# Pooling maxima through DRAM instead of a diagonal and a product with ones, and a new list of pieces

## The chip, the cores and the metric

One core of a Trainium2 chip runs the whole program. The metric is device time in microseconds of one execution; a kernel is told by the median of its runs. Engines: TensorE (PE, its weight loads PEld), VectorE (DVE), ScalarE (ACT), GpSimd (POOL) and SyncE (SP), which issues nearly all DMA transfers.

## The reference

Attention with pooled keys and values for 8 batches of 8 heads, then a two-layer network on the 4608 rows of its result:

```python
a = softmax(phi, axis=2)                    # phi: 8 x 8 x 576 x 32
k_m = einsum('bhsm,bhsd->bhmd', a, k)       # 32 pooled keys a head
v_m = einsum('bhsm,bhsd->bhmd', a, v)
attn = softmax(q @ k_m.T / sqrt(64)) @ v_m  # over the 32
x = attn as 4608 x 512
h = x @ w_in                                # 512 x 2048
out = (h - tanh(h)) @ w_out                 # 2048 x 512
```

The program's softmax of phi first needs, for each of the 256 columns (8 heads of 32) of a batch, the maximum over the 576 positions: it is subtracted from phi ahead of the exponential.

## The kernel before, in words

The work is cut into pieces, and a string, ORDER, lists every piece by hand or by a planner as a word; a loop runs through it, and each engine gets its instructions in just that order. A word is a letter for the step, then its indices; a step of several parts (Python `yield`) is named once for each part. "i0:gg", "o3:gg", "k1:q" are loads of blocks of w_in, w_out, or of a block to be checked, into a buffer whose name stands behind the colon. A trailing x takes the other PSUM buffer. SP's transfers too are issued in the list's order: an issue waits until the buffer is free and until the data are there, and what stands behind it on SP waits with it.

The words that matter here, with b a batch, t a half of its positions, u a unit of 256 rows, f a fourth of the 2048 columns:

- FX b, FQ b load phi with columns on partitions (`pt`), FA b loads it with positions on partitions (`e`); KA, KB, KR load keys and values, Q, QT load queries.
- X b: VectorE takes the maxima `mx` (128 partitions x 2) of `pt`. For batches 0 and 1 another way is used, which the change leaves alone. For batches 2 to 7 it also makes `dg`, the identity times the maxima (L193).
- XP b: TensorE multiplies ones by `dg` (L202), which puts the 256 maxima into every partition of a PSUM tile, `pmx`.
- Y b (batches 2, 3) subtracts `pmx` from `e` on VectorE (L210, L213); YM b (batches 4 to 7) copies it to SBUF as `ms` on ScalarE (L221) and subtracts on GpSimd. YE b is the exponential on ScalarE (L226).
- V b pools keys and values with `e` (L271, L279), N b divides, U b and UV b turn the result; S b.t are the scores, AM, AE, AD, AT, AS the second softmax and its split into a high and a low f16 half (L351 to L564); a "v" behind AM, AD, AS, c, s, L, SS or CW (and Ev) moves a step from GpSimd or ScalarE to VectorE.
- P b.f folds the pooled values into w_in (L573); H u.f is the first layer's product (L622); a or ap, g, c, f, s turn it into f16 parts of h - tanh(h) (L629 to L693); M u.f is the second layer's product (L750 for the first units, L769 for the rest), E or Ev adds up and stores.
- T p turns blocks of float64 weights, read as integers, into f32 and f16 on VectorE (L447, L450, L453) and ScalarE (L464); L, Lv, Lp make the low half. Z are products that only keep TensorE busy.

Of the kernel before, what the change touches and what calls it, by code (L numbers as in the profile page):

```python
# [83 lines left out]
AMv2.0 PL1.3 M0.2 L14 c1.3 c0.3 H2.2 H2.2 AMv2.0 AM2.1 AM2.1 a2.2 AE2.0 ADv2.0 P2.0 a2.2 H2.3 H2.3 a2.3 M1.2 M1.2 PL2.0 a2.2 BF0 g2.2 cv2.2 H3.2 L15
P2.1 H3.2 L14 M1.3 a2.3 a2.3 BH0 BL0 M1.3 ADv2.0 W2 AT2.0 ap3.2 P2.1 R1 O1 O1 AE2.1 ap3.2 ap3.2 PL2.1 BS1 BF1 AS2.0 AS2.0 M0.3 M0.3 H4.0 H4.0 ap4.0 R0
P2.2 H3.3 g2.3 c2.3 O0 O0 BH1 BL1 AD2.1 AD2.1 ap4.0 ap4.0 M2.2 R2 X3 g3.2 c3.2 P2.2 PL2.2 H3.3 H4.1 H4.1 ap3.3 ap3.3 g4.0 ap4.1 ap4.1 KR3.0 XP3 Y3
f4.0 s4.0 M2.2 QT3.0 ap3.3 g3.3 s4.0 YE3 cv4.0 M2.3 M2.3 H4.2 O2 O2 c3.3 ap4.1 AT2.1 R3 H4.2 BS2 P2.3 AS2.1 P2.3 g4.1 AS2.1 V3.0x PL2.3 ap4.2 ap4.2
BF2 BH2 M3.2 f4.1 ap4.2 f4.2 M3.2 H4.3x s4.1 KR3.1 s4.1 BL2 V3.1 N3 k4:q XX M3.3 M3.3 H4.3 ap4.3 ap4.3 g4.2 U3x U3 UV3 M4.0 M4.0 cv4.1 UV3 S3.0x ap4.3
O3 O3 P3.0 M4.0 M4.0 S3.0 AMv3.0 P3.0 M4.1 H5.0 BS3 AMv3.0 AE3.0 f4.3 k0:e g4.3 cv4.3 M4.1 M4.1 M4.1 PL3.0 c4.2 s4.2 s4.2 P3.1 H5.0 a5.0 a5.0 M4.2
sv4.3 H5.1 CW4 BF3 a5.0 BH3 BL3 H5.1 g5.0 k2:q c5.0 M4.2 M4.2 f5.0 QT3.1 M4.2 H5.2 s5.0 sv4.3 M4.3 P3.1 a5.1 ADv3.0 a5.1 M4.3 M4.3 PL3.1 S3.1 ADv3.0  # L90
s5.0 a5.1 AT3.0 M4.3 H5.2 S3.1 E4 g5.1 a5.2 a5.2 E4 CW2 f5.1 E4 E4 sv5.1 P3.2 M4.3 H5.3 H5.3 FQ4 M5.0 FA4 M5.0 a5.2 cv5.1 E4 E4 AS3.0 a5.3 sv5.1 M5.0
M5.0 CW0 AS3.0 H6.0 M5.1 M5.1 M5.1 M5.1 f5.2 a5.3 g5.2 KR4.0 cv5.2 s5.2 s5.2 a5.3 H6.0 a6.0 f5.3 a6.0 a6.0 P3.2 H6.1 s5.3 H6.1 f6.0 M5.2 M5.2 M5.2
M5.2 P3.3 g5.3 c5.3 s5.3 M5.3 ap6.1 ap6.1 PL3.2 H6.2 ap6.1 g6.1 P3.3 AM3.1 AM3.1 c6.1 AE3.1 X4 XP4 g6.0 M5.3 c6.0 s6.0 PL3.3 f6.1 H6.2 a6.2 KR4.1 M5.3
Ev5 Ev5 M5.3 s6.0 Ev5 Ev5 Ev5 a6.2 ADv3.1 ADv3.1 YM4 M5.3 s6.1 Ev5 a6.2 YM4 YE4 H6.3 H6.3 s6.1 QT4.0 AT3.1 ap6.3 ap6.3 M6.0 M6.0 AS3.1 AS3.1 g6.2 k3:e
f6.2 M6.0 sv6.2 V4.0 M6.1 M6.1 ap6.3 g6.3 f6.3 M6.0 M6.1 M6.1 sv6.3 sv6.2 H7.0 H7.0 a7.0 c6.2 V4.1 N4 W3 a7.0 sv6.3 M6.2 SI0 H7.1 a7.0 f7.0 H7.1 a7.1
U4 UV4 FQ5 UV4 M6.2 QT4.1 M6.2 a7.1 M6.2 U4 H7.2 H7.2 SSv0 NI0 a7.1 f7.1 a7.2 c6.3 M6.3 NI0 g7.0 a7.2 a7.2 s7.0 S4.0 c7.0 S4.0 AMv4.0 M6.3 M6.3 E6
s7.0 g7.2 c7.2 H7.3 H7.3 E6 a7.3 M6.3 E6 s7.1 E6 E6 W4 g7.1 M6.3 E6 s7.1 P4.0 P4.0 S4.1x S4.1 AMv4.1 a7.3 X5 CW3 AMv4.0 AE4.0 a7.3 g7.3 M7.0 M7.0 M7.0
M7.0 H8.0 H8.0 f7.2 c7.1 M7.1 M7.1 M7.1 M7.1 s7.2 f7.3 PL4.0 ap8.0 ap8.0 AMv4.1 AD4.0 ap8.0 XP5 s7.2 k5:e sv7.3 CW5 cv7.3 M7.2 KR5.0 AD4.0 f8.0 g8.0
M7.2 M7.2 M7.2 sv7.3 AE4.1 ADv4.1 s8.0 s8.0 c8.0 AT4.0 H8.1 YM5 ADv4.1 H8.1 P4.1 P4.1 M7.3 M7.3 a8.1 a8.1 a8.1 H8.2 AS4.0 PL4.1 M7.3 Ev7 H8.2 a8.2 FA5
QT5.0 YM5 a8.2 YE5 f8.1 M7.3 Ev7 P4.2 P4.2 g8.1 M7.3 AS4.0 c8.1 s8.1 s8.1 Ev7 Ev7 a8.2 g8.2 Ev7 H8.3 M8.0 Ev7 M8.0 c8.2 M8.0 V5.0 M8.1 AT4.1 AS4.1  # L100
KR5.1 PL4.2 H9.0 H8.3 a8.3 a8.3 a8.3 H9.0 f8.2 a9.0 a9.0 s8.2 s8.2 M8.1 M8.1 V5.1 f8.3 P4.3x P4.3 N5 s8.3 k6:e M8.0 M8.1 g8.3 H9.1x H9.1 a9.0 PL4.3
U5x s8.3 UV5 ap9.1 f9.0 M8.2 M8.2 UV5 ap9.1 ap9.1 c8.3 f9.1 M8.2 M8.2 M8.3 g9.0 c9.0 M8.3 SI1 k7:q SS1 U5 S5.0 g9.1 M8.3 sv9.0 k8:e E8 E8 H9.2 E8 E8
S5.0 M8.3 M8.3 AS4.1 H9.2 H9.3x sv9.0 CW6 ap9.2 ap9.2 ap9.2 QT5.1 c9.1 M9.0 M9.0 M9.0 E8 E8 s9.1 s9.1 AM5.0 H9.3 a9.3 AM5.0 f9.2 a9.3 FQ6 a9.3 NI1x
NI1 AE5.0 AD5.0 AD5.0 H10.0x H10.0 M9.1 M9.1 a10.0 s9.2 P5.0 f9.3 S5.1x a10.0 g9.2 P5.0 c9.2 a10.0 M9.0 M9.1 H10.1 s9.2 CW8 M9.1 M9.2 g9.3 c9.3 S5.1
AMv5.1 AMv5.1 AE5.1 M9.2 M9.2 M9.2 AT5.0 AS5.0 X6 XP6 s9.3 H10.1 s9.3 M9.3 PL5.0 ap10.1 H10.2 AS5.0 ADv5.1 ap10.1 ap10.1 g10.1 f10.1 g10.0 YM6 f10.0
H10.2 a10.2 FA6 P5.1 P5.1 c10.0 CW7 YM6 PL5.1 M9.3 a10.2 a10.2 QT6.0 M9.3 M9.3 M9.3 s10.0 E9 E9 s10.1 H10.3x KR6.0 H10.3 H11.0 cv10.1 a10.3 E9 E9 E9
E9 a10.3 a10.3 YE6 P5.2 P5.2 s10.0 M10.0 M10.0 M10.0 KR6.1 V6.0 H11.0 PL5.2 a11.0 H11.1 k10:q a11.0 s10.1 f10.2 s10.2 M10.0 M10.1 g10.2 a11.0 H11.1
# [1033 lines left out]
```

## Time and profile before

| | |
|---|---|
| median of 3 runs | 635.8 us (635.18 to 636.08) |
| the profiled execution | 636.29 us, span 634.2 us |
| busy, share of the span | PE 98%, DVE 90%, ACT 68%, POOL 55% |
| mean granted TensorE clock | 0.996 |

A row tells a line of the kernel, the engine, the operation, tiles written <- tiles read, and shape. Busy times of matmuls overlap their neighbours, so a product's place in TensorE's queue is read from the start of the next one.

### The profile page before, as it was taken

To read this page: it belongs to the slowest core of one execution; us is meant where nothing else is said; L and a number is where in the kernel's file an instruction comes from. 1 tells how busy PE (TensorE), PEld (TensorE's weight loads), DVE (VectorE), ACT (ScalarE), POOL (GpSimd) and SP (SyncE) were. 2 spreads that over 40 slices of the span, in tenths; PEclk is the share of its full clock that TensorE was granted. 3 is DMA by queue.
4 is the path that set the end of the run, shared out by engine and by line. 5 is a ranking of instruction groups with operands and counts; after the bars stand their busy time and mean duration, and the time that the engine had idled before them with its cause. 6 is when DMAs were issued, how large, how long until landed. Compare 5 with 4: busy or idle time off the path is not lost.

```text
span 634.2 us, 16291 instructions
## 1 busy us (share of the span) xinstructions
PE 619.4 (98%) x6908; PEld 485.5 (77%) x6908; DVE 570.9 (90%) x763; ACT 428.7 (68%) x601; POOL 350.5 (55%) x314
## 2 busy tenths in 40 slices
...
GB/s 342 416 269 274 252 264 158 118 73 68 184 138 145 65 56 72 73 167 112 116 85 122 113 67 149 109 88 173 38 41 163 118 103 89 49 153 35 166 100 39
DMA packets 25872, 85.03 MB, mean 134 GB/s; under 512 B 2752, under 2 KB 2752, under 8 KB 25024
## 3 DMA queue, kind: packets, MB, share of 16 engines
...
HBM read 72.37 MB, written 11.53 MB: 132 GB/s over the span
## 4 chain that ended last, share of the span: by engine, by line
PE 86%; DVE 7%; DMA 4%; ACT 1%; issue 1%; SPq 0%; DVEq 0%; ACTq 0%
PE h L622 27%; PE x L769 22%; PE o L769 16%; PE o L750 10%; PE pp L573 3%; PE o1h L750 3%; DMA raw<-in_w_out_dram 3%; PE pkv L271 2%; DMA pt<-in_phx_dram 1%; PE psc L323 1%; DVE h L642 1%; DVE wt L450 1%; DVE wt L453 1%; DVE h L646 1%; DVE bw L709 0%
## 5 line engine op out<-in xcount | busy, mean ns | idle before, releaser
L622 PE MATMUL h<-ah,ph 128*128 128x256 f16 (+3 forms) x1536 | 201.0, 246 | 0.7 <-DVE h L642 0.7
L622 PEld LDWEIGHTS <-ph 128*128 128x128 f16 x2304 | 178.2, 98 | 20.7 <-issue 3.7
L672 POOL TENSOR_TENSOR g<-h,g 128x512 f16<-128x512 f32 x114 | 128.3, 1147 | 100.4 <-ACT g L666 94.2
L622 PE MATMUL h<-al,ph 128*128 128x256 f16 (+3 forms) x768 | 170.0, 246 | 1.1 <-POOL al L564 1.1
L693 POOL TENSOR_TENSOR f<-s,f 128x512 f16<-128x512 f32 x86 | 107.3, 1269 | 86.1 <-ACT f L689 81.1
L769 PEld LDWEIGHTS <-f 128*128 128x128 f16 x1344 | 129.1, 98 | 20.8 <-issue 5.2
L769 PE MATMUL x<-bt,f 128*128 128x256 f16 x1008 | 128.3, 273 | 0.0
L644 ACT ACTIVATE u<-u,beta 128x1024 f32<-128x1024 f32 x72 | 82.5, 1146 | 46.8 <-DVE h L642 46.5
L769 PEld LDWEIGHTS <-g 128*128 128x128 f16 x1008 | 97.9, 98 | 14.7 <-issue 3.5
L629 ACT ACTIVATE u<-h 128x1024 f32<-128x1024 f32 x72 | 73.3, 1018 | 47.6 <-PE h L622 31.4
L642 DVE SCALAR_TENSOR_TENSOR h<-h,u 128x1024 f32<-128x1024 f32 x72 | 87.9, 1221 | 19.2 <-ACT u L629 17.6
L646 DVE SCALAR_TENSOR_TENSOR h<-u,h 128x1024 f32<-128x1024 f32 x72 | 92.7, 1289 | 11.7 <-ACT u L644 11.4
L666 ACT ACTIVATE g<-h 128x512 f16<-128x512 f32 (+2 forms) x128 | 68.2, 579 | 19.9 <-DVE h L646 13.4
L750 PEld LDWEIGHTS <-g 128*128 128x128 f16 x384 | 36.7, 98 | 45.2 <-issue 3.0
L689 ACT ACTIVATE f<-s 128x1024 f16<-128x1024 f32 x56 | 58.6, 1048 | 11.1 <-DVE s L682 7.0
L750 PE MATMUL o<-wout_hi,g 128*128 128x512 f16 x192 | 59.0, 379 | 0.0
L680 DVE TENSOR_TENSOR s<-h 128x512 f32<-128x512 f32 x56 | 45.3, 808 | 2.0 <-DVE h L646 0.5
L769 PE MATMUL o<-wout_hi,f 128*128 128x256 f16 x224 | 45.9, 273 | 0.0
L769 PE MATMUL o<-wout_hi,g 128*128 128x256 f16 x224 | 45.8, 273 | 0.0
L769 PE MATMUL x<-wout_hi,g 128*128 128x256 f16 x224 | 45.8, 273 | 0.0
L769 PE MATMUL o<-bt,g 128*128 128x256 f16 x336 | 45.3, 273 | 0.0
L586 ACT ACTIVATE ph<-pp 128x1024 f16<-128x1024 f32 x32 | 32.4, 1014 | 18.4 <-PE pp L573 17.6
...
## 6 DMA issues: line engine op xcount, KB each, us to landing
...
chk<-in_w_in_dram SPq DMA_DIRECT2D x16, 512.0 KB, 4.1
chk<-in_w_out_dram SPq DMA_DIRECT2D x16, 512.0 KB, 3.8
...
kv<-in_kva_dram SPq DMA_DIRECT2D x6, 1032.0 KB, 9.7
...
raw<-in_w_out_dram SPq DMA_DIRECT2D x12, 512.0 KB, 8.6
```

The lines of the kernel that those rows point to most:

```text
L622: nc.tensor.matmul(hp[:, k, tu : tu + w], px[:, g, cs], d[ax][:, g, ta : ta + w], start=(n == 0), stop=(n == 5),)
L629: nc.scalar.activation(uu, hp, AF.Square, scale=1.0 / (S_A * S_P))
L642: nc.vector.scalar_tensor_tensor(t, hp, C2 * S_G / (S_A * S_P), uu, op0=ALU.mult, op1=ALU.mult)
L644: nc.scalar.activation(uu, uu, AF.Square, bias=c["beta"])
L646: nc.vector.scalar_tensor_tensor(h3, uu, CC, t, op0=ALU.add, op1=ALU.mult)
L666: nc.scalar.activation(hi, x, AF.Copy)
L672: eng.tensor_tensor(lo[:, ks], x[:, ks], hi[:, ks], op=ALU.subtract)
L680: nc.vector.tensor_tensor(s[:, 0:2], pair, a_block(h3, 0, 0).unsqueeze(1).to_broadcast((P, 2, 2, P)), op=ALU.add)
L689: nc.scalar.activation(f[:, 0], s, AF.Copy)
L693: eng.tensor_tensor(f[:, 1, ks], s[:, ks], f[:, 0, ks], op=ALU.subtract)
L750: nc.tensor.matmul(o, gx[:, k, P * tt : P * tt + P], wx[:, 4 * fb + k, :], start=(first and k == 0 and wx is wout_hi and gx is gh), stop=( ...
L769: nc.tensor.matmul(dst, a(na, kk), b(nb, kk), start=(new and kk == 0 and na == 0 and nb == 0), stop=(end and kk == 1 and na == 1))
```

## The change

The maxima of batches 2 to 7 go to a DRAM tile of 2 x 128, and from there to all partitions of an SBUF tile `ms` of their own; the diagonal, the product with ones, its PSUM tile and ScalarE's copy go. Y and YM both subtract `ms`. Both transfers are issued by SP, at X and at XP.

```diff
-        dg = big.tile([P, 2, P], F32, tag="qt", name=f"dg{b}", bufs=1)
-        nc.vector.tensor_tensor(
-            dg, self.c["ident"].unsqueeze(1).to_broadcast((P, 2, P)),
-            mx.unsqueeze(2).to_broadcast((P, 2, P)), op=ALU.mult,
-        )
-        d["dg"] = dg
-
-    def top_all(self, b, d, early=False):
-        nc, dg = self.tc.nc, d["dg"]
-        pa = self.psum(f"pmx{b}", early)
-        nc.tensor.matmul(pa[:, 0, 0:256], self.c["ones"], dg.rearrange("p a b -> p (a b)"), start=True, stop=True)
-        d["px"] = pa
+        d["md"] = self.dram.tile([2, P], F32, tag=f"md{b}", name=f"md{b}")
+        nc.sync.dma_start(d["md"].rearrange("r p -> p r"), mx)
+
+    def top_all(self, b, d):
+        d["ms"] = m = self.big.tile([P, 256], F32, tag="ms", name=f"ms{b}", bufs=1)
+        row = d["md"].rearrange("r p -> (r p)").unsqueeze(0).to_broadcast((P, 256))
+        self.tc.nc.sync.dma_start(m, row)
...
-    def expo(self, b, d):
-        self.less_top(self.tc.nc.vector, d["e"], d["px"][:, 0, 0:256])
-
-    def expo_pool(self, b, d):
-
-        m = self.big.tile([P, 256], F32, tag="qt", name=f"ms{b}", bufs=1)
-        self.tc.nc.scalar.activation(m, d["px"][:, 0, 0:256], AF.Copy)
-        yield
-        self.less_top(self.tc.nc.gpsimd, d["e"], m)
+    def expo(self, b, d, eng=None):
+        self.less_top(eng or self.tc.nc.vector, d["e"], d["ms"])
```

The list is replaced as a whole (1710 words before, 1707 after). The same pieces are in it; many stand elsewhere, and some have moved between engines. To VectorE: AS 0.0, 1.0, 2.0, 2.1, 3.1, 6.1, 7.1; AM 1.1, 3.1, 6.0, 6.1; AD 1.1, 5.0, 6.1; L2, SS1; c 2.0, 7.2, 8.1, 10.2, 11.3, 12.0, 12.1 and eight s. Away from it: AS 7.0; AM 2.0, 4.0; AD 2.0, 3.1; L4, L7; c 0.1, 4.0, 4.1, 5.1, 7.3, 10.1, 12.3, 14.3, 16.0 and seven s; E5, E7, E11 for E4 and E15. From the start of the second batch's softmax, and around batch 2's maxima, it reads:

```diff
-H0.0x ASv0.1 T10 ASv0.1 H1.0 Lp9 T10 T10 L10 o6:gg o7:gg H1.1 H0.0
+ASv0.0 ASv0.0 o6:gg H0.0x AT0.1 Lp9 T10 ASv0.1 ASv0.1 H1.0 H1.1 Z0.0 Z0.0 H0.0 KA1 o7:gg T10 T10 T11 T11 FX1 X1
...
-AT1.1 T5 OP1 OP1 FA2 T5 T4 L5 L5 Q2.0 H2.0x H2.0 cv0.1 M0.1 AS1.1 T4 KB2 M0.1 T4 T4 PL1.1 H2.1 FX2 a2.0 a2.0 X2 XP2 o8:gg AS1.1 H3.0 OP0 OP0 H2.1 a2.0
-g2.0 M2.0 i12:kv2 T12 T12 T12 Y2 a2.1 CW1 H3.0 c2.0 T12 a2.1 Lv4 o11:gg T13 T13 P0.2 P0.2 M2.0 a2.1 H3.1 i14:kv3 g2.1 KA2 c2.1 ap3.0 FA3 PL0.2 YE2
-Lv12 ap3.0 ap3.0 V2.0 V2.1
+OP1 OP1 T5 T5 T4 L5 PL1.0 L5 ASv1.0 H2.0 H2.0 T4 T4 OP0 FA2 M0.1 FX2 X2 PL1.1 H2.1x ap2.0 o10:pp5 XP2 Q2.1 T4 ap2.0 L4 o11:gg H2.1 AS1.1 H3.0 OP0 L4
+P0.2 T12 T12 T12 ap2.0 g2.0 M2.0 H3.1 a2.1 Y2 a2.1 a2.1 cv2.0 H3.0 g2.1 KA2 a3.0 P0.2 PL0.2 T13 YE2 V2.0 V2.1
```

## Rows read from the trace of the kernel before

**Rows 1.** The page of the profile: span and instructions; busy time, share of the span and instructions of each engine; and the chain that ended last, its shares by engine.

```profile
span 634.2 us, 16291 instructions
...
PE 619.4 (98%) x6908; PEld 485.5 (77%) x6908; DVE 570.9 (90%) x763; ACT 428.7 (68%) x601; POOL 350.5 (55%) x314
...
PE 86%; DVE 7%; DMA 4%; ACT 1%; issue 1%; SPq 0%; DVEq 0%; ACTq 0%
```

**Rows 2.** Busy time of each engine (with the number of instructions) in four stretches of the span; after them the granted TensorE clock, the DMA engines' mean busy share and GB/s.

```profile
0.00:60.00 60.00, 51.31 (x522) 28.70 (x522) 49.46 (x80) 38.55 (x51) 17.76 (x28) 0.97 0.83 326
60.00:200.00 140.00, 140.00 (x1457) 86.42 (x1456) 136.70 (x162) 91.80 (x112) 73.73 (x55) 1.00 0.44 154
200.00:560.00 360.00, 358.73 (x4309) 308.51 (x4294) 327.58 (x439) 252.53 (x371) 223.15 (x199) 1.00 0.31 104
560.00:634.20 74.20, 69.31 (x639) 61.89 (x637) 57.16 (x85) 45.79 (x69) 35.87 (x34) 0.99 0.25 87
```

**Rows 3.** The timeline of TensorE's matmuls around three of the XP products (start, us; us until the end of the last one merged; line, operation, tiles, shape, count).

```profile
83.17 0.62 PE L202 MATMUL pmx<-dg,ones 128*128 128x256 f32 x2
83.63 0.27 PE L622 MATMUL h<-ah,ph 128*128 128x256 f16 x1
83.74 0.27 PE L622 MATMUL h<-al,ph 128*128 128x256 f16 x1
...
169.52 0.65 PE L202 MATMUL pmx<-dg,ones 128*128 128x256 f32 x2
170.00 0.38 PE L750 MATMUL o<-wout_hi,g 128*128 128x512 f16 x1
...
448.78 0.60 PE L202 MATMUL pmx<-dg,ones 128*128 128x256 f32 x2
449.21 0.38 PE L769 MATMUL x<-bt,f 128*128 128x256 f16 x2
```

**Rows 4.** The chain that ended last in the first 80 us, its two long loads (start, us); and the timeline from 22 to 40 us (an idle time before an instruction and what ended it in brackets).

```profile
10.43 14.39 DMA raw<-in_w_out_dram
...
40.51 5.65 DMA raw<-in_w_out_dram
...
22.83 0.16 DVE L284 TENSOR_SCALAR kr<-pkv 128x2 f32<-128x2 f32 x1 [2.07 <-PE pkv L279]
...
36.07 1.39 POOL L564 TENSOR_TENSOR al<-af,ah 128x576 f16<-128x576 f32 x1 [0.36 <-ACT ah L562]
...
37.51 0.27 PE L622 MATMUL h<-al,ph 128*128 128x256 f16 x1 [1.11 <-POOL al L564]
...
34.97 1.36 DVE L447 TENSOR_SCALAR wt<-raw 128x512 uint32<-128x512 uint32 x2
36.24 0.77 DVE L373 STREAM_TRANSPOSE af<-sc 128x576 f32<-128x576 f32 x1
36.94 1.67 DVE L450 SCALAR_TENSOR_TENSOR wt<-raw,wt 128x512 uint32<-128x512 uint32 x2
38.53 0.75 DVE L564 TENSOR_TENSOR al<-af,ah 128x576 f16<-128x576 f32 x1
```

**Rows 5.** Groups of TensorE's matmuls, shapes apart: count, busy us, mean ns of one, idle time before.

```profile
L858 PE MATMUL warm<-nid 128*128 128x512 f16 x52 | 13.7, 411 | 1.9 <-DVE nid L1086 1.9
```

**Rows 6.** Instructions by tile: the diagonal dg, the exponential on e and the copy ms (duration in ns min/median/max, first and last start).

```profile
L193 DVE TENSOR_TENSOR dg<-ident,mx x6: 424/444/1099, 80.5 to 440.0; 128x256 f32<-128x256 f32 x6
...
L226 ACT ACTIVATE e<-e x6: 1147/1147/1164, 93.2 to 469.0; 128x1152 f32<-128x1152 f32 x6
...
L221 ACT ACTIVATE ms<-pmx x4: 363/364/384, 258.2 to 449.4; 128x256 f32<-128x256 f32 x4
```

**Rows 7.** DMA issues (count, KB each, median us from issue to landing), and the times to landing of all stores to out_dram.

```profile
kv<-in_kva_dram SPq DMA_DIRECT2D x6, 1032.0 KB, 9.7
...
raw<-in_w_out_dram SPq DMA_DIRECT2D x12, 512.0 KB, 8.6
...
DMA to landing us min/median/max: 2.0/2.3/6.9
```

**Rows 8.** The timeline around batch 2's maxima: SP's issue of KA2, VectorE's maximum and subtraction, TensorE where V2.0 begins.

```profile
81.58 1.40 SPq L161 DMA_DIRECT2D kv<-in_kva_dram  x1
...
79.09 1.34 DVE L191 TENSOR_REDUCE mx<-pt 128x2 f32<-128x1152 f32 x1
...
85.02 1.22 DVE L210 TENSOR_TENSOR e<-e,pmx 128x1024 f32<-128x1024 f32 x1
86.15 0.58 DVE L213 TENSOR_TENSOR e<-e,pmx 64x128 f32<-64x128 f32 x2
...
95.02 1.98 PE L271 MATMUL pkv<-kv,e 128*32 128x129 f32 x64
```

**Rows 9.** Instructions of four lines on VectorE and GpSimd: the attention's split (L564), its first subtraction (L353), a sum of two SBUF tiles (L681), the low half of the weights (L475).

```profile
L564 POOL TENSOR_TENSOR al<-af,ah x14: 1274/1283/1464, 36.1 to 551.7; 128x576 f16<-128x576 f32 x14
...
L564 DVE TENSOR_TENSOR al<-af,ah x2: 747/795/843, 38.5 to 523.1; 128x576 f16<-128x576 f32 x2
...
L353 DVE TENSOR_TENSOR sc<-sc,sm x6: 745/990/1339, 134.9 to 518.0; 128x576 f32<-128x576 f32 x6
...
L681 DVE TENSOR_TENSOR s<-s,h x56: 424/426/1269, 174.4 to 618.6; 128x256 f32<-128x256 f32 x56
...
L475 DVE SCALAR_TENSOR_TENSOR win_lo<-wt,win_hi x4: 1216/1218/1223, 19.5 to 111.8; 128x1024 f16<-128x1024 f32 x4
```

More of the change, by code (lines that the diff above doesn't have):

```diff
@@ L84 @@
[L84 to L107, printed above, removed]
@@ L132 @@
-M17.3 GX M17.2 M17.3 M17.3 M17.2 M17.3 WD E17 E17 E17 E17 E17 E17
+Z0.0 Z0.0 Z0.0 Z0.0 Z0.0 i1:gg i0:gg T0 Z0.0 Z0.0 T0 T0 T0 Z0.0 Z0.0 i6:kv3 T3 Z0.0 Z0.0 FX0 X0 Z0.0 i3:pp5 Z0.0 YX0 T3 T3 Z0.0 Z0.0 Z0.0 Lp0 Lp0 XU0
+Z0.0 i2:gg T3 T1 T1 T1 i4:kv2 T2 T2 Lp3 T2 T1 KB0 KA0 XT0 XT0 XU0 Z0.0 Lv1 T2 Z0.0 o2:gg Lp3 Z0.0 Z0.0 V0.0 V0.1 Lv2 N0 U0x U0 Z0.0 o3:gg Z0.0 Q0.0
+S0.0x T9 T9 T9 S0.0 UV0 UV0 T9 AM0.0 AM0.0 Q0.1 S0.1 S0.1 AM0.1 AM0.1 P0.1x P0.1 P0.0 AE0.0 AD0.0 P0.0 PLp0.1 AE0.1 o9:pp4 AD0.1 PLp0.1 PLp0.0 PLp0.0
@@ new lines @@
+OP1 OP1 T5 T5 T4 L5 PL1.0 L5 ASv1.0 H2.0 H2.0 T4 T4 OP0 FA2 M0.1 FX2 X2 PL1.1 H2.1x ap2.0 o10:pp5 XP2 Q2.1 T4 ap2.0 L4 o11:gg H2.1 AS1.1 H3.0 OP0 L4
+P0.2 T12 T12 T12 ap2.0 g2.0 M2.0 H3.1 a2.1 Y2 a2.1 a2.1 cv2.0 H3.0 g2.1 KA2 a3.0 P0.2 PL0.2 T13 YE2 V2.0 V2.1 T13 P1.2x a3.0 T12 a3.0 H3.1 P1.2
+i12:kv2 g3.0 c2.1 Lv12 T6 T13 T13 T6 PL1.2 M2.0 M2.1 OP2 i14:kv3 a3.1 a3.1 T6 T6 Lv13 k1:q CW1 M2.1 a3.1 g3.1 H0.2 H0.2 T7 T7 N2 OP2 H1.2 H1.2 T7 T7
+M3.0 ap0.2 U2 UV2 c3.0 c3.1 Lv6 L7 L7 BS0 ap1.2 ap0.2 ap0.2 M3.0 M3.1 ap1.2 ap1.2 g0.2 c0.2 P0.3x P0.3 OP3 M3.1 OP3 PL0.3 g1.2 c1.2 UV2 H0.3 o12:kv2
@@ new lines @@
+T14 T14 o14:kv3 H0.3 H1.3 H1.3 M0.2 FA3 U2 S2.1x T15 T15 a0.3 a0.3 T15 a1.3 T14 T15 L15 L15 Q2.0 S2.0 a0.3 S2.0 FQ3 g0.3 c0.3 S2.1 AM2.1 P1.3x P1.3
+M0.2 a1.3 AM2.0 T14 L14 H2.2 H2.2 AM2.0 AE2.0 PL1.3 a1.3 g1.3 L14 P2.0 P2.0 c1.3 H2.3 a2.2 X3 M1.2 M1.2 M1.3 a2.2 H3.2 AD2.0 AD2.0 H2.3 AM2.1 a2.2
+g2.2 a2.3 a2.3 M1.3 AT2.0 ASv2.0 BF0 BH0 BL0 P2.1 ASv2.0 H3.2 AE2.1 cv2.2 P2.1 PL2.0 a2.3 g2.3 M0.3 ap3.2 ap3.2 P2.2 H4.0 H4.0 M0.3 R1 O1 O1 P2.2 H3.3
+M2.2 PL2.1 XP3 H4.1x W2 c2.3 ap3.2 g3.2 c3.2 BS1 M2.2 AD2.1 BF1 M2.3 R0 O0 O0 BH1 ap4.0 ap4.0 QT3.0 H3.3 KR3.0 PL2.2 M2.3 ap4.0 ap3.3 BL1 Y3 H4.1 f4.0
@@ new lines @@
+R2 ap3.3 P2.3 g4.0 ap4.1 ap4.1 ap3.3 O2 ap4.1 f4.1 c4.0 AD2.1 AT2.1 YE3 V3.0x ASv2.1 H4.2 O2 g3.3 c3.3 XX BS2 P2.3 M3.2 sv4.0 PL2.3 H4.2 ap4.2 M3.2
+sv4.0 ap4.2 ap4.2 sv4.1 KR3.1 V3.1 R3 BF2 BH2 f4.2 ASv2.1 g4.1 H4.3 c4.1 sv4.1 M3.3 M3.3 H4.3 ap4.3 ap4.3 FQ4 N3 U3 U3 BL2 O3 M4.0 ap4.3 S3.0x k4:q
+UV3 UV3 P3.0 g4.2 X4 S3.0 AMv3.0 AMv3.0 O3 M4.0 BS3 f4.3 H5.0 H5.0 a5.0 M4.0 M4.0 s4.2 M4.1 M4.1 M4.1 P3.0 a5.0 PL3.0 a5.0 BF3 g4.3 c4.2 M4.1 AE3.0
+cv4.3 f5.0 CW4 sv4.3 sv4.3 P3.1 P3.1 s4.2 BH3 BL3 PL3.1 M4.2 H5.1 H5.1 a5.1 ADv3.0 ADv3.0 s5.0 M4.2 M4.2 QT3.1 S3.1 S3.1 M4.2 k0:e CW0 g5.0 c5.0 M4.3
@@ new lines @@
+a5.1 QT4.0 H5.2 H5.2 a5.1 f5.1 g5.1 c5.1 ap5.2 M4.3 AT3.0 M4.3 Ev4 Ev4 M4.3 M4.3 ap5.2 ap5.2 W3 s5.1 Ev4 AS3.0 H5.3x H5.3 s5.0 M5.0 M5.0 Ev4 M5.0 Ev4
+Ev4 M5.0 a5.3 f5.2 AS3.0 H6.0x a5.3 a5.3 k2:q f5.3 FA4 s5.1 M5.1 M5.1 M5.1 M5.1 H6.0 P3.2 s5.2 a6.0 s5.2 g5.2 cv5.2 a6.0 a6.0 P3.2 s5.3 s5.3 g5.3 H6.1
+H6.1 AMv3.1 c5.3 AMv3.1 M5.2 P3.3 P3.3 PL3.2 M5.2 M5.2 ap6.1 g6.0 c6.0 M5.3 f6.0 ap6.1 ap6.1 M5.2 s6.0 PL3.3 XP4 g6.1 M5.3 f6.1 KR4.0 AE3.1 YM4 AD3.1
+AD3.1 CWv2 H6.2 M5.3 M5.3 H6.2 ap6.2 s6.0 KR4.1 E5 sv6.1 E5 AT3.1 E5 ap6.2 ap6.2 ASv3.1 ASv3.1 M5.3 E5 H6.3x E5 E5 YE4 H6.3 M6.0 M6.0 a6.3 a6.3 f6.2
@@ new lines @@
+c6.1 k3:e FQ5 M6.0 QT4.1 V4.0 a6.3 s6.2 g6.3 c6.3 M6.0 sv6.1 H7.0 H7.0 s6.2 f6.3 g6.2 c6.2 M6.1 M6.1 M6.1 a7.0 a7.0 a7.0 V4.1 N4 f7.0 H7.1 H7.1 U4
+s6.3 s6.3 UV4 a7.1 UV4 a7.1 a7.1 M6.2 M6.2 U4 SI0 SSv0 f7.1 H7.2 H7.2 ap7.2 M6.1 M6.2 M6.2 s7.0 s7.0 g7.0 c7.0 NI0 M6.3 NI0 ap7.2 ap7.2 f7.2 M6.3 M6.3
+E6 M6.3 E6 E6 E6 S4.0x H7.3x g7.1 c7.1 s7.1 s7.1 CWv3 M7.0 X5 H7.3 a7.3 g7.2 S4.0 M6.3 E6 E6 a7.3 s7.2 s7.2 M7.0 AM4.0 AM4.0 P4.0 cv7.2 S4.1x S4.1
+AMv4.1 AMv4.1 AE4.1 M7.1 M7.0 H8.0 P4.0 M7.0 M7.1 a7.3 M7.1 M7.1 g7.3 c7.3 M7.2 M7.2 H8.1 f7.3 H8.0 k5:e CWv5 M7.2 s7.3 FA5 a8.0 PL4.0 a8.0 a8.0 M7.2
```

85 lines of the change are left out of this document (45 added, 40 removed).

## The prediction

> **What bounds the kernel now.** I read first the shares of busy time and the times [rows 1]: TensorE is busy 98% of the span, VectorE 90%, ScalarE 68%, GpSimd 55%. A share says nothing about where it is lost, so next came the busy time by stage [rows 2]: TensorE is busy 51.31 of the first 60 us, all of the 140 us from 60 to 200, 358.73 of the 360 us to 560, and to the end but for some 5 us. The granted clock is 1.00 (the 2.4 GHz level) from 60 to 560 us, so no clock term enters. A busy TensorE need not be one that streams, so I looked at single starts [rows 3]: products of 256 columns in f16 start 0.11 us apart without a hole, there and nearly everywhere after 60 us. From 60 us on the kernel is as long as TensorE's list of products. The chain of waits says the same, PE 86% and DVE 7% [rows 1]. Before 60 us it is another kernel: the chain runs through two loads of w_out (14.39 and 5.65 us) and through VectorE's conversions between them [rows 4], and TensorE fills its time with 13.7 us of warm-up products [rows 5]. So one microsecond of product removed after 60 us should shorten the run by one, and so should one taken from the conversions before 54 us.
>
> VectorE is the second bound: 136.70 of the 140 us from 60 to 200 [rows 2], against 327.58 of the next 360.
>
> **What is removed.** Each XP was one f32 product of 128x256, shown as two matmuls. What it takes from TensorE's list is the start of the next product less its own first start: 83.63 - 83.17 = 0.46, 170.00 - 169.52 = 0.48, 449.21 - 448.78 = 0.43 us [rows 3]; six times 0.46 is 2.8 us. VectorE loses six diagonals of 0.44 us, 2.7 us; ScalarE loses four copies of 0.36 us, 1.5 us [rows 6]. Only the products lie on the path. PSUM buffer pa is no longer held from XP to Y; TensorE showed no wait for it, so that is worth nothing.
>
> **What is added.** Two SP transfers per batch: 256 elements of 4 bytes to DRAM, then 1 KB read by each of 128 partitions. No row shows either. Bounds from the rows on landing [rows 7]: below, the fastest store, 2.0 us for 256 KB; above, 8.6 us, the median of the w_out loads while the queues are full. The write of 1 KB is nearest the stores and the read moves 128 KB, so I take 2 to 4 us each; both ends are kept. Issue is 0.33 to 0.43 us of SP's time. The Trainium skill, DMA: Bandwidth & Descriptors, Rules for kernel authors, says that a non-contiguous last dimension becomes one descriptor per element and that transfers under 64 KB are mostly overhead; its fixed 2.0 us would make the pair 4 us by estimate, and no run here shows it.
>
> Who waits? SP holds everything behind X until VectorE's maximum, and behind XP until the write has landed. Of the new list I counted the product time between places (H 2.65, a unit's M 5.2 or 4.6 us). Batch 2 is the tight one. X2 stands 2.6 us of products earlier than before; between it and V2.0 are now 12.2 us, before 11.8. Behind X2 and XP2 on SP stand o10, Q2.1, o11, KA2. Before, the maximum ran 79.09 to 80.4, KA2 left at 81.58 and V2.0 started at 95.02 [rows 8]. Now the maximum should end at 80.4 - 2.6 = 77.8 and V2.0 is due at 95.0 - 2.2 = 92.8 (its place is 2.2 us of products earlier). Two strings must meet that. Exponentials: 77.8 + two issues (0.7) + write w + read r + subtraction 1.8 + exponential 1.15 [rows 6, 8] = 81.5 + w + r, free up to w + r = 11.3 us, and 2 to 4 each is far below. KA2: 77.8 + issue 0.35 + w + three issues (1.2) + 9.7 for landing [rows 7] = 89.1 + w, free up to w = 3.7, and 0.3 us late at w = 4. I take no stall. Batches 3 to 7 have 20 to 52 us of products between X and the subtraction; in the list XP4 and XP5 stand right ahead of it, but SP has nothing to wait for after FA4, FA5 and QT5.0, 15 and 6 us earlier. They cost nothing. Removing dg and ms from buffer qt also lets QT loads leave earlier; with TensorE without idle time from 60 to 200 us and 1.3 us of it to 560 [rows 2], that is worth nothing.
>
> **What moves.** The list is new, and the numbers of products and warm-ups are the same but for XP. Halves change engine, seven splits from GpSimd (1.28 us) to VectorE (0.80) and one back, and so on [rows 9]. From 60 to 200 us VectorE gains three more splits, one subtraction and one division (about 3.9 us) and c2.0 (1.2), and loses AM2.0, AD2.0 (1.5), Lv4 and Lv7 (2.4), c0.1 (1.2) and two diagonals (0.9): 0.9 us less. Later it gains about 2 us where 32 are free. Both hidden beside TensorE.
> In the start-up one move lies on the path. The low half of batch 0's first attention went on GpSimd, 36.07 to 37.46, with TensorE held 1.11 us; now VectorE does it, 0.75 us [rows 4, 9], in a stretch where it has no gap, ahead of the conversion that frees the buffer of the load of w_out at 40.5. Bounds: 0.75 us later (all of it on the conversions' chain) to 0.3 us earlier (GpSimd's 1.39 exchanged for a conversion's 1.36 ahead of it and 0.75). I take +0.4. Lv2 (1.22 us, [rows 9]) now precedes N0, while VectorE waited 2.07 us there for TensorE: nothing.
> The tail of the list is the same.
>
> **Sum.** Profiled execution 636.29 (span 634.2 and 2.1 around it): 636.29 - 2.8 + 0.4 = 633.9. It was 0.49 above the median of the runs shown, 635.8, so the median after is 633.4, or -0.4%. A change under 0.2% (1.3 us) is about what a measurement of this kernel can't tell from none.
>
> **Rivals.**
> *VectorE sets the pace from 60 to 200 us.* For: 97.6% busy there. Then two products removed there, 0.9 us, come back as waits. Y2 and Y3 make it worse: they read ms from SBUF now, where pmx was in PSUM. The rows show what two SBUF inputs can cost beside GpSimd: L681 takes 0.426 us mostly but up to 1.269, L353 0.745 to 1.339 [rows 9]. Six such instructions, 0.84 each, are at most 5.0 us against 3.3 free and 0.9 relieved: 0.8 us over. Time: 633.4 + 0.9 + 0.8 = 635.1, within 0.2%. Against: GpSimd is busy 73.73 of these 140 us [rows 2], so about half should meet it.
> The Trainium skill, SBUF — State Buffer, section SBUF: two separate sides, says that VectorE with two SBUF inputs and GpSimd take a shared pair of ports by exclusive lock, the loser blocked for the whole instruction; by that rule each of the six would be blocked or not as the list falls. The trace agrees as far as those maxima go.
>
> *The path through DRAM is slow (the other side).* Place: SP at X2 and XP2. If both transfers queue among the loads of that stretch at the upper bound, w = r = 8.6: exponentials 81.5 + 17.2 = 98.7, KA2 89.1 + 8.6 = 97.7, against 92.8: TensorE stalls 5.9 us, 633.4 + 5.9 = 639.3. It eats the gain and 1.3 us more from w + r = 11.3 + 3.7 = 15.0 us, or w = 7.4. For: the loads around it took 8 to 10 us. Against: they move 500 to 1000 times the write's bytes.
>
> *The new list is better by itself.* TensorE lost 8.7 us idle and 13.7 on warm-ups in the first 60 us and 1.3 idle to 560 [rows 2, 5]. A tenth of the first, 2.2, and the 1.3, and no loss at the start (0.4), give 633.4 - 3.9 = 629.5; half of that 631.5. I price it at 631.
>
> **Numbers.** Forecast 0.58, VectorE 0.16, DRAM path 0.14, better list 0.12. Of the forecast's own range, 632.2 to 634.8, a little lies within 0.2% (above 634.5): faster 0.53 + 0.12 + 0.03 = 0.68; same 0.05 + 0.13 = 0.18; slower 0.14. The range reaches from 630.6 (most of the better lists) to 636.0 (over the VectorE case), and leaves out the DRAM case and the extreme lists, some 0.19.
>
> **What would show it.** Right: no f32 product of 128x256 by ones; TensorE's busy time down by about 3 us; the first w_out product of unit 0 at 54 to 55 us; V2.0 without a wait for kv or e; the writes landing in 2 to 4 us; TensorE without idle time from 60 to 200. Wrong: TensorE waiting for kv, e or POOL's subtraction after an XP; TensorE gaps from 60 to 200 that end with a VectorE instruction of two SBUF inputs; a first M0.0 over 1 us from 54.

## The result and the profile after

The kernel after takes 639.45 us, the kernel before, on the same chip, 635.49: a ratio of 1.0064, 95% interval 1.0051 to 1.0077. It is slower by 0.6%, where 633.4 us was forecast. The profiled execution has a span of 637.6 us, 3.4 more than before.

First the page of the kernel after: busy time by engine, and the chain that ended last.

```profile
span 637.6 us, 16252 instructions
...
PE 617.4 (97%) x6896; PEld 483.2 (76%) x6896; DVE 568.4 (89%) x764; ACT 431.6 (68%) x598; POOL 333.9 (52%) x304
...
PE 83%; DVE 8%; DMA 4%; ACT 2%; issue 1%; SPq 1%; POOL 0%; ACTq 0%; DVEq 0%
```

Against [rows 1], TensorE has 12 matmuls less and 2.0 us less to do: what was to be removed is gone. Yet it is now 97% busy instead of 98%. The next view says where: the busy time of each engine in the stretches of [rows 2].

```profile
0.00:60.00 60.00, 50.61 (x530) 28.70 (x538) 51.64 (x84) 37.00 (x46) 12.13 (x24) 1.00 0.82 323
60.00:200.00 140.00, 134.27 (x1376) 81.45 (x1374) 127.63 (x148) 93.51 (x113) 68.46 (x50) 0.99 0.46 157
200.00:560.00 360.00, 359.79 (x4332) 308.16 (x4331) 328.16 (x446) 252.30 (x368) 214.76 (x197) 1.00 0.33 102
560.00:637.60 77.60, 72.69 (x670) 64.92 (x668) 60.99 (x89) 48.76 (x74) 38.57 (x36) 1.00 0.28 97
```

From 200 to 560 us TensorE is as full as before. All of the loss lies from 60 to 200 us: 134.27 busy of 140, where there had been no idle time; VectorE fell from 136.70 to 127.63 with it, so a full VectorE is not the reason. The list of what TensorE waited for in that stretch has one row (waited for, us, times, longest):

```profile
PE o L738 <- ACT g L654: 5.7, 1, 5.7
```

One wait of 5.7 us. The timeline around it, by engine (start, us; in brackets the idle time before and what ended it): SP's issues, ScalarE, VectorE, TensorE.

```profile
78.03 0.38 SPq L193 DMA_DIRECT2D md<-mx  x1
78.46 0.46 SPq L418 DMA_DIRECT2D raw<-in_w_out_dram  x1
87.39 0.33 SPq L198 DMA_DIRECT2D ms<-md  x1
...
88.72 0.55 SPq L161 DMA_DIRECT2D kv<-in_kva_dram  x1
...
79.45 0.33 ACTq L823 DMA_DIRECT2D d<-ot  x1
...
84.09 0.59 ACT L821 ACTIVATE ot<-o 128x512 f32<-128x512 f32 x1
90.72 0.33 ACTq L823 DMA_DIRECT2D d<-ot  x1
91.15 1.06 ACT L654 ACTIVATE g<-h 128x1024 f16<-128x1024 f32 x1 [6.46 <-DMA raw<-in_w_out_dram]
...
92.65 1.23 DVE L205 TENSOR_TENSOR e<-e,ms 128x1024 f32<-128x1024 f32 x1 [7.05 <-DMA ms<-md]
...
92.26 0.61 PE L738 MATMUL o<-wout_hi,g 128*128 128x512 f16 x1 [5.73 <-ACT g L654]
92.66 0.63 PE L738 MATMUL o<-wout_lo,g 128*128 128x512 f16 x1
...
99.81 1.98 PE L259 MATMUL pkv<-kv,e 128*32 128x129 f32 x64
```

The write of the maxima leaves at 78.03; SP can't issue the read (87.39) before it has landed, 9.3 us later. The load of w_out issued behind it at 78.46 lands at 90.65, after 12.2 us, and ScalarE's store d, issued at 79.45, at 91.29, after 11.8 us. In the kernel before, the two such loads of this stretch took 4.1 and 5.0 us; the stores just ahead of the write took 2.0. The nearest comparison is run 8 below, with the same order of transfers and a write of another form: 7.2 us for the load and 6.8 for the store. ScalarE's second store then can't be issued until 90.72: its issue waits on the completion semaphore that this late load of w_out used last, as the trace's semaphore events have it. Behind the store in ScalarE's queue stands g of unit 2, and for g TensorE waits 5.73 us. VectorE stood for 7.05 us too, for ms, but it is not named in TensorE's wait.

From 92 to 94 us the granted clock is 0.50, the 1.2 GHz level, behind an idle time of TensorE of 5.7 us: the products of 512 columns start 0.4 us apart (92.26, 92.66) until 95 us and 0.21 afterwards. Seven products at 0.2 more each are 1.4 us. The sum 634.2 - 2.8 + 5.7 + 1.4 = 638.5 is 0.9 over the span of 637.6; from 200 to 560 us TensorE's idle time fell from 1.27 us to 0.21, which is as much. The pooling products V2.0 start at 99.81, where the forecast's count had them at 92.8.

The same stretch, busy time by engine; the last three columns are the granted clock, the mean busy share of the DMA engines and GB/s:

```profile
78.00:80.00 2.00, 2.00 (x11) 0.90 (x10) 2.00 (x2) 1.60 (x3) 2.00 (x2) 1.00 0.22 33
80.00:82.00 2.00, 2.00 (x36) 1.80 (x34) 2.00 (x5) 2.00 (x3) 0.25 (x1) 1.00 0.00 0
82.00:84.00 2.00, 2.00 (x28) 1.90 (x26) 2.00 (x4) 1.69 (x2) 1.06 (x1) 1.00 0.19 49
84.00:86.00 2.00, 2.00 (x33) 1.55 (x38) 1.60 (x2) 0.69 (x2) 1.33 (x1) 1.00 0.12 29
86.00:88.00 2.00, 0.53 (x24) 0.03 (x8) 0.00 (x0) 0.00 (x0) 0.00 (x0) 1.00 0.44 35
...
92.00:94.00 2.00, 1.74 (x5) 0.64 (x6) 1.35 (x2) 2.00 (x3) 0.00 (x0) 0.50 1.01 413
```

A load of 512 KB and a store of 256 KB stand open, and the engines move 0 to 49 GB/s until the write lands at 87.4. By the packet records the write's 256 packets of 4 bytes were taken up within a third of a microsecond, 9 ns each; what is slow comes behind that. The store's first packet starts at 89.0, after the write has landed. So the write is not only late itself: it holds the others. The trace tells the landing of four of the six writes and five of the six reads (one line by tile each, the writes first; min, median, max from issue to landing). By the last completion events the other writes took 9.3 us (batch 2) and 7.7 (batch 6), and the other read 6.0 (batch 5).

```profile
DMA to landing us min/median/max: 7.7/9.3/9.7
DMA to landing us min/median/max: 4.6/5.1/5.5
```

### The profile page after: what moved, and what is told of

The parts are those of the page before. It is cut to its first block, busy times and chain, and to the rows that moved or that the text cites. A ratio compares the mean times of both kernels' runs of the same rounds, so it can differ in the third digit from the quotient of the medians.

```text
span 637.6 us, 16252 instructions
## 1 busy us (share of the span) xinstructions
PE 617.4 (97%) x6896; PEld 483.2 (76%) x6896; DVE 568.4 (89%) x764; ACT 431.6 (68%) x598; POOL 333.9 (52%) x304
## 2 busy tenths in 40 slices
DMA packets 28368, 85.82 MB, mean 135 GB/s; under 512 B 4480, under 2 KB 5248, under 8 KB 27520
## 4 chain that ended last, share of the span: by engine, by line
PE 83%; DVE 8%; DMA 4%; ACT 2%; issue 1%; SPq 1%; POOL 0%; ACTq 0%; DVEq 0%
PE h L610 26%; PE x L757 22%; PE o L757 17%; PE o L738 8%; PE pp L561 3%; DMA kv<-in_kva_dram 3%; PE pkv L259 2%; DMA raw<-in_w_out_dram 2%; PE o1h L738 2%; DVE wt L441 1%; PE psc L311 1%; DVE h L630 1%; DVE wt L438 1%; DVE wt L435 1%; DVE h L634 1%
## 5 line engine op out<-in xcount | busy, mean ns | idle before, releaser
L660 POOL TENSOR_TENSOR g<-h,g 128x512 f16<-128x512 f32 x118 | 130.8, 1130 | 120.4 <-ACT g L654 93.6
L681 POOL TENSOR_TENSOR f<-s,f 128x512 f16<-128x512 f32 x84 | 103.5, 1253 | 75.4 <-ACT f L677 75.3
```

The lines of the kernel that those rows point to most:

```text
L660: eng.tensor_tensor(lo[:, ks], x[:, ks], hi[:, ks], op=ALU.subtract)
L681: eng.tensor_tensor(f[:, 1, ks], s[:, ks], f[:, 0, ks], op=ALU.subtract)
```

## The experiments

Theory A: the write of the maxima is what costs. A1 says that it costs by holding the other transfers, A2 that it costs only those who wait for ms. Rival B: the new list is slower by itself. Rival C: any small transfer would take as long among these loads. All ratios are to the kernel before on the same chip, with a 95% interval; its median there was 635.88 to 635.95 us, 0.4 over the chip of the result.

**1. The list with the old path** (XP2, XP3, XP6 and XP7 stand a few words away, where the buffer pa is free).

```
-        d["md"] = ...; nc.sync.dma_start(d["md"].rearrange("r p -> p r"), mx)
+        d["dg"] = dg = big.tile([P, 2, P], F32, tag="dg", ...)   # and the product of before
...
+        nc.tensor.matmul(pa[:, 0, 0:256], self.c["ones"], d["dg"]..., start=True, stop=True)
+        self.tc.nc.scalar.activation(m, pa[:, 0, 0:256], AF.Copy)
```

> The new list with the old path (diagonal, product with ones, ScalarE's copy to ms at once; XP2, XP3, XP6 and XP7 moved by a few places so that the buffer pa is free for it). Theory A, the path through DRAM costs the time: the forecast of 633.4 us was right but for the stall of batch 2, so this is 633.4 + 2.8 for the six products = 636.2, at most 637; no wait of ScalarE or TensorE of 5 us around 86 to 92 us. Rival B, the new list is slower by itself: 639.45 + 2.8 = 642, at least 640.

Measured: 656.46 us, 1.0327 (1.031 to 1.0345). That is far over A's 637; it meets B's "at least 640" by the letter, but TensorE's waits name my edit's own operations:

```profile
PE pmx L201 <- DVE dg L193: 3.6, 1, 3.6
PE h L614 <- ACT ms L202: 3.0, 2, 2.6
```

The product comes at places where VectorE has the diagonal not yet ready, and ScalarE's copy holds pa. This list has no room for the old path, and the run says nothing about the list alone. From 60 to 560 us TensorE waits 15.3 us, and 8.7 of them are at the product or for the copy. These don't make up the whole 20 us; the rest I leave open.

**2. The path with the old list** (its second YM word does the subtraction).

> The list of before, with the path through DRAM. Theory A: before's list gives batch 2 less room, VectorE's subtraction stood 85.02 us, 4.6 us after the maximum ends at 80.4; with 9.3 + 5.2 us for write and read it starts at about 95.6, so VectorE waits some 10 us and the time is 635.5 - 2.8 + 6 to 10 = 639 to 643. Rival B, the new list is what costs: 635.5 - 2.8 = 632.7, at most 634.

Measured: 679.06 us, 1.0678 (1.0659 to 1.0697). B as the only cause falls, and A's figure was too small by far. Before's list has batch 2's XP right behind X, so SP issues the read with nothing in between and stands still while the write lands (79.93 to 89.58). From 60 to 200 us VectorE waited 14.5 us for a load of w_out, 11.0 for ms, and TensorE 13.5 for the low half of the weights:

```profile
DVE wt L439 <- DMA raw<-in_w_out_dram: 14.5, 1, 14.5
PE pp L565 <- DVE win_lo L467: 13.5, 1, 13.5
DVE e L205 <- DMA ms<-md: 11.0, 1, 11.0
```

So the new list is made around the new path; the two parts can't be priced one by one.

**3. Batch 2 alone by the old path.**

```
     def top(self, b, d):
...
+        if b == 2:
+            d["dg"] = dg = ...      # diagonal, and in top_all the product and the copy
+            return
         d["md"] = self.dram.tile([2, P], F32, ...)
```

> The kernel after, with batch 2 alone on the old path (XP2 placed right ahead of H2.1). Theory A, the loss lies in batch 2, whose write of 4-byte elements lands after 9.3 us: TensorE's 5.7 us at M2.0's place goes and one product of 0.46 comes back: 639.45 - 5.7 + 0.5 = 634.2, between 633.2 and 635.2. If the five later writes cost as well, by what they hold up: 636 to 638. Rival B, the list: 639.9, no change beyond the product.

Measured: 636.81 us, 1.0017 (1.0004 to 1.0029). The wait for ScalarE's g is gone and 2.6 us with it, less than forecast: the copy cost TensorE 2.2 us in its place.

```profile
PE h L623 <- ACT ms L207: 2.2, 1, 2.2
```

The copy was late because this run takes SP's waits for batch 2 away as well. The loads of q, w_out, keys and values leave at 72.2 to 74.1 us, the store d issued at 73.84 lands after 8.4 us, and ScalarE waits 2.7 us for that store's buffer right ahead of the copy. So the run doesn't price the write alone; run 5 shows the same collision.

**4. The same path with large elements.** VectorE turns a 32-column tile in blocks, and two writes of 4 rows of 128 bytes go out.

```
-        nc.sync.dma_start(d["md"].rearrange("r p -> p r"), mx)
+        nc.vector.transpose(mt[:, 1], mt[:, 0])
+        for r in range(2):
+            nc.sync.dma_start(d["md"][r].rearrange("(k x) -> k x", x=32), mt[r::32, 1])
```

> The kernel after, with the maxima turned on the chip before they are written: VectorE transposes a 32-column tile in blocks of 32 (one short instruction more), and two writes of 4 rows of 128 bytes each take the place of 256 elements of 4 bytes. Theory A, the number of elements makes the write slow and holds the other transfers: the writes land in 2 to 4 us, the loads around them in under 10, no 5 us wait: 632.9 to 634.5. Rival C, any small write among these loads waits for them: landing stays 7 to 10 us and the time 638 to 640.

Measured: 634.7 us, 0.9982 (0.9971 to 0.9993). C falls: in batch 7 the second write is issued at 441.24 and the read, which waits for both, at 442.82, so they land within 1.6 us. The reads stay slower, 3.5 to 6.5 us by the completion events and 6.5 in batch 2, and VectorE waits 1.2 us for that one.

**5. No exchange at all, the new list alone.**

```
-        nc.sync.dma_start(d["md"].rearrange("r p -> p r"), mx)
-        d["ms"] = m = ...; self.tc.nc.sync.dma_start(m, row)
+        d["ms"] = self.c["ms0"]
```

> The kernel after without the exchange of maxima: nothing is written and nothing read, the subtraction takes zeros from a tile set once (so the maxima are left out of the exponentials). What is left is the new list alone. Theory A, the exchange costs what the forecast missed: 633.4 us less what VectorE no longer waits for, 632.5 to 634. Rival B, the list is slower by itself: 638 or more.

Measured: 636.63 us, 1.0011 (0.9997 to 1.0025): no gain. This was meant as the price of the list and is not. Without the waits at X and XP, SP sends the loads of q, w_out, keys and values at 70.8 to 72.8 us, some 16 us earlier than in the kernel after, and they meet ScalarE's stores d, which land after 8.9 and 9.6 us instead of 2.0. ScalarE then waits for a buffer ot, and TensorE behind it:

```profile
81.39 0.60 ACT L817 ACTIVATE ot<-o 128x512 f32<-128x512 f32 x1 [3.23 <-DMA d<-ot]
...
84.51 1.22 DVE L630 SCALAR_TENSOR_TENSOR h<-u,h 128x1024 f32<-128x1024 f32 x1 [1.94 <-ACT u L628]
86.37 1.23 DVE L626 SCALAR_TENSOR_TENSOR h<-h,u 128x1024 f32<-128x1024 f32 x1 [0.63 <-ACT u L613]
...
87.64 0.41 PE L557 MATMUL pp<-win_hi,vh 64*32 64x512 f16 x8 [2.66 <-DVE h L626]
```

Behind this idle time the granted clock falls too, to 0.53 from 90 to 92 us. SP's wait for the maximum had kept these loads back. A wait taken away let loose a transfer that collides.

**6. The writes, but nobody reads them.**

```
-        d["ms"] = m = ...; self.tc.nc.sync.dma_start(m, row)
+        d["ms"] = self.c["ms0"]
```

> The kernel after with its six element-wise writes, but no read: the subtraction takes zeros, so nobody waits for the writes to land (the maxima are left out of the exponentials). Theory A1, the write's 256 elements hold the DMA engines and with them ScalarE's store d of unit 0, whose late completion is what TensorE waits for: 638 to 640, the 5.7 us wait for ScalarE's g stays. Theory A2, VectorE's wait for ms is what costs: as the run without exchange, 632.5 to 634, the wait is gone although the store still lands after 10 us or more.

Measured: 639.78 us, 1.006 (1.0046 to 1.0074): as slow as the kernel after, with no wait for ms. A2 falls. But the 5.7 us wait for g did not stay as A1 had it; two waits share the loss, for g behind the late store and for the key and value load:

```profile
89.60 0.39 PE L736 MATMUL o<-wout_hi,g 128*128 128x512 f16 x1 [2.02 <-ACT g L652]
98.59 1.65 PE L257 MATMUL pkv<-kv,e 128*32 128x129 f32 x52 [2.75 <-DMA kv<-in_kva_dram]
```

The second is what A1 says: the load was issued at 80.97, behind the write, and landed after 17.5 us, where it took 10.1 in run 5. The first is a third way that neither theory had: ScalarE's second store is issued at 88.06 because its issue waits on the completion semaphore that the write itself used last, and the write lands at 87.98. So something still waits for a write that nobody reads: the next transfer that takes its semaphore.

**7. 128 pairs instead of 256 elements.** In DRAM the two maxima of a partition lie side by side; the subtraction reads every second number.

```
-        nc.sync.dma_start(d["md"].rearrange("r p -> p r"), mx)
+        nc.sync.dma_start(d["md"], mx)                  # d["md"] is [P, 2]
...
+            y = m.rearrange("p (x r) -> p r x", r=2).unsqueeze(1).to_broadcast((P, n, 2, 128))
```

> The kernel after with the maxima written as 128 pairs of 8 bytes instead of 256 elements of 4, and read with the subtraction taking every second number. If the write's time goes by elements (9.3 us for 256): it lands after 4.7 us, ms 5 us later, VectorE waits some 2.5 us at most and the time is 634 to 636. If it has a fixed length whatever the number: 639.5, no change.

Measured: 634.08 us, 0.9974 (0.9962 to 0.9987). The six writes land after 2.8 to 4.7 us, ms after 4.0 to 5.9, and VectorE waits 0.6 us.

**8. Pairs in batch 2 alone** (the later five as in the kernel after).

```
+        shape, turn = ([P, 2], "p r -> p r") if b == 2 else ([2, P], "r p -> p r")
```

> The kernel after, with 128 pairs of 8 bytes in the write of batch 2 alone; the five later writes stay element by element and land after 8 to 9.7 us. If only batch 2's place is tight, this is as fast as the run with pairs in all batches: 634.1, within 633.4 and 634.9. If the five later writes cost too by what they hold up: 635 to 638.

Measured: 633.68 us, 0.9966 (0.9953 to 0.9979): the lowest median of all, though its interval overlaps that of run 7, and 5.8 us under the kernel after, by one write. With a short write the new list is faster than the kernel before, so rival B is out. The five others land after up to 9.9 us, and nothing waits there. TensorE's wait for g has shrunk to 0.73 us, and V2.0 starts at 93.67, 0.9 from the forecast's 92.8:

```profile
87.43 0.39 PE L741 MATMUL o<-wout_hi,g 128*128 128x512 f16 x1 [0.73 <-ACT g L657]
93.67 1.98 PE L262 MATMUL pkv<-kv,e 128*32 128x129 f32 x64
```

**9. The turned maxima with batch 2's subtraction two words later.**

> The kernel with turned maxima, and batch 2's subtraction two places later, behind the two last instructions of a2.1: VectorE does 1.2 us of work where it waited 1.2 us for ms. If VectorE sets TensorE's pace there, 634.7 - 1.2 = 633.5; if not, unchanged at 634.7; above 635 if the exponential then comes late for the pooling products.

Measured: 638.01 us, 1.0039 (1.0026 to 1.0052). The time is that of the third case, but not its reason: VectorE no longer waited for ms, the exponential was not late, and TensorE still waited at V2.0 (92.2 to 94.8).

```profile
PE pkv L261 <- ACT u L634: 2.6, 1, 2.6
```

```profile
90.37 1.16 ACT L216 ACTIVATE e<-e 128x1152 f32<-128x1152 f32 x1 [0.53 <-DVE e L210]
```

```profile
88.89 1.44 DVE L210 TENSOR_TENSOR e<-e,ms 64x128 f32<-64x128 f32 x2
90.36 2.07 DVE L662 TENSOR_TENSOR g<-h,g 128x1024 f16<-128x1024 f32 x1
```

The u that the wait names had itself waited 2.1 us for VectorE. Moved, the end of the subtraction and the g behind it ran beside a GpSimd instruction (89.00 to 91.35) and took 1.44 and 2.07 us, where they took 0.58 and 1.22 in run 4: 1.7 us more on VectorE, and V2.0 starts 1.6 us later than in run 4 (94.80 and 93.20).

**10. The write's own price.** The kernel before gets one write that nobody reads, from a constant tile, so that nothing else is changed; three sizes.

```
     def top_all(self, b, d, early=False):
+        if b == N_ROWS and ...:                          # N_ROWS is 2
+            md = self.dram.tile([2, P], F32, ...)        # b_128: [P, 2], written as it is
+            nc.sync.dma_start(md.rearrange("r p -> p r"), self.c["ident"][:, 0:2])   # b_512: twice
```

> The kernel before, with one write more on SP's queue where batch 2's product with ones stands: 128 pairs of 8 bytes from a constant tile to a place in DRAM that nobody reads; it waits for nothing and nobody waits for it. It should leave at about 77.2 us, behind the load of 76.8, and land after some 3.7 us, at 81, when the next loads leave. Theory A1 (while such a write runs, the DMA engines do little else): 635.9 to 636.9. Rival A2 (it costs only who waits for it): 635.9.

> As before, but 256 elements of 4 bytes. Theory A1: it holds the engines from about 77.2 to 86.6, the loads and the store that leave at 81 lose some 5.5 us, the key and value load lands at 96 to 97 instead of 91.1 to 91.7 and the pooling products, 95.02 before, start 2 to 5 us later: 638 to 641. Rival A2: 635.9, and the load's landing stays at about 91.

> As before, but two such writes, 512 elements of 4 bytes. Theory A1: the engines are held twice as long, to about 96, and the key and value load lands at about 106: 11 us or so of stall, 645 to 649. Rival A2: 635.9.

Measured: 128 pairs 635.81 us, 0.9997 (0.9988 to 1.0005); 256 elements 637.91, 1.0039 (1.0026 to 1.0052); 512 elements 640.62, 1.0071 (1.0049 to 1.0093). The write left earlier than I had thought, at 71.3 to 72.1 us. Landing (line by tile), 128 pairs, 256 and 512 elements:

```profile
DMA to landing us min/median/max: 4.9/4.9/4.9
```

```profile
DMA to landing us min/median/max: 9.4/9.4/9.4
```

```profile
DMA to landing us min/median/max: 9.5/9.6/9.8
```

256 elements cost 2 us though nobody reads them. The key and value load lands at 94.65, not 91.09, but nothing waits for it. What TensorE waits for from 60 to 200 us is ScalarE's g (256 elements, then 512):

```profile
PE o L754 <- ACT g L670: 1.0, 1, 1.0
```

```profile
PE o L756 <- ACT g L672: 2.8, 1, 2.8
```

With 256 elements the two stores d beside the write took 9.0 and 9.8 us, where they had taken 3.6 and 4.0 before, and ScalarE had to wait for their buffer: A1 again, by the stores. But two writes side by side landed together after 9.5 to 9.8 us, where twice the time was expected, and the loss was 4.7 us, not 9 to 13. So the time does not go by the number of elements alone.

**11. Number or neighbours.** The same write into the kernel before: 256 elements 64 bytes apart in DRAM, 512 bytes apart, and 128 elements side by side.

```
+            md = self.dram.tile([2, P, 16], F32, ...)    # 128 for 512 bytes
+            nc.sync.dma_start(md[:, :, 0].rearrange("r p -> p r"), self.c["ident"][:, 0:2])
...
+            md = self.dram.tile([1, P], F32, ...)        # b_col
+            nc.sync.dma_start(md.rearrange("r p -> p r"), self.c["ident"][:, 0:1])
```

> The kernel before with one write of 256 elements of 4 bytes from a constant tile, as in b_256, but each element 64 bytes from the next in DRAM. If the time goes by the number of elements in a transfer: lands after 9.4 us, 637.9. If it comes from small elements that lie side by side in DRAM: lands after 5 us or less, 635.9.

> As b_apart64, with the elements 512 bytes apart. By the number: 9.4 us and 637.9. By neighbours in DRAM: 2 to 5 us and 635.9; if 64 bytes are too near but 512 are not, this run alone is short.

> The kernel before with one write of 128 elements of 4 bytes from one column of a constant tile, side by side in DRAM (512 bytes in all). By the number of elements: half of 256, 4.7 us, as the 128 pairs of 8 bytes took (4.9), 635.9. By neighbours: as many elements lie within each 64 bytes as in b_256, so 9.4 us and 637.9.

Measured: 64 bytes apart 635.6 us, 0.9996 (0.9986 to 1.0005); 512 apart 635.64, 1.0001 (0.9991 to 1.0011); 128 side by side 637.19, 1.0016 (1.0004 to 1.0028), with executions from 635.87 to 637.97; the one profiled took 635.9, so its trace shows the landing and not the loss. Landing, in this order:

```profile
DMA to landing us min/median/max: 3.6/3.6/3.6
```

```profile
DMA to landing us min/median/max: 3.5/3.5/3.5
```

```profile
DMA to landing us min/median/max: 8.4/8.4/8.4
```

It is the neighbours, not the number: 256 elements lying apart land in 3.6 us, and 128 of 4 bytes side by side take 8.4, where 128 pairs of 8 bytes took 4.9. Each 64 bytes of DRAM took sixteen writes in the slow runs, eight with pairs, and one with elements 64 bytes apart; which block of DRAM it is that counts, no run tells. The two stores d took 5.3 and 4.9 us beside the elements 64 bytes apart, against 9.8 and 9.0 beside the same number side by side (run 10): what holds the others goes with the form of the write too.

## Why the prediction was wrong

**The step that failed** is the write's size: "The write of 1 KB is nearest the stores and the read moves 128 KB, so I take 2 to 4 us each". In batch 2 they took 9.3 and 5.2 us. The nearest row by bytes was the wrong one: those stores have rows of 2 KB, the write has elements of 4 bytes beside each other. The upper bound, 8.6 us from the median of the loads, was under the truth too.

**The conditions built on it were right.** The sum said that the exponentials are free up to w + r = 11.3 us and the key and value load up to w = 3.7; 14.5 and 9.3 were measured. Its landing was put at 89.1 + w, which with w = 9.3 is 98.4, and it landed at 98.48. The rival "path through DRAM is slow" gave 639.3 us at a chance of 0.14; 639.45 came.

**But not by that rival's place.** It had TensorE wait at V2.0 for SP's late load or the exponentials. TensorE in fact waited 6 us sooner, at ScalarE's g, because the write held the load of w_out, and with it the semaphore that ScalarE's store needed. Only run 6 shows part of the loss at V2.0. Yet the rival's place stood close behind: V2.0 started at 99.81 and could not have before 98.48, when the key and value load landed. By these two figures, an estimate, the wait for g and the slow clock cost 1.3 us beyond what V2.0 would have lost anyway, and that the rival's number is so near is in part luck: its 8.6 us each were 9.3 and 5.2. I had asked who is queued behind the write on SP, and not what else runs on the same DMA engines: the added transfer was priced as if it took nothing from the others.

**Right:** the products. With a short write (run 8) the span is 631.9, against 634.2 - 2.8 = 631.4 by the sum's largest term; the time is 633.68, the forecast 633.4. That it is so close is in part luck: run 8 has two waits from 60 to 200 us that the sum lacks, 1.0 us together, and from 200 to 560 us it is idle for 0.13 us where the kernel before was for 1.27. Batches 3 to 7 cost nothing, as said: run 8 leaves their slow writes and loses nothing.

**Not decided:** the start-up, +0.4. M0.0 starts at 53.80 against 54.01 before, with VectorE at the low half at 36.09 as foreseen and TensorE still waiting 1.0 us for it. But in the traces of runs 10 and 11, whose start-up is that of the kernel before, M0.0 starts anywhere from 52.92 to 54.42, so single traces can't tell a loss of 0.4 from none.

**VectorE as the pace** did not show in the kernel after. The mechanism named for it is there: of the two subtractions from SBUF one took 1.23 us, with GpSimd idle, and one 1.80, beside a GpSimd instruction. In run 9 VectorE lost 1.7 us the same way.

The Trainium skill, DMA: Bandwidth & Descriptors, Rules for kernel authors, was cited with one descriptor per element and a fixed 2.0 us. The first agrees: packets under 512 bytes rose from 2752 to 4480, by 1728, of which 6 x 256 = 1536 are the elements. The second stands in another section of that page, Anatomy of one DMA — SWDGE (gpsimd) path, and is given for transfers that GpSimd issues; these writes, issued by SP, took 7.7 to 9.7 us, so it could not be carried over. The same page, Specifications, says that transfers under 512 bytes make the DMA read, modify and write; runs 10 and 11 agree in that small pieces side by side are slow, but 4-byte pieces lying apart landed in 3.5 us, and what happens inside no run here shows.
